# Causal attention in a fused kernel: 64x64 blocks and array tiles in place of full 128x128 blocks

## Chip, cores and metric

The kernel runs on one core of one Trainium2 chip. The metric is device time in microseconds (us), median of several runs. TensorE is called PE, VectorE DVE, ScalarE ACT, GpSimd POOL, and SyncE, which issues the DMA transfers, SP.

## What is computed

Three layers, one after the other, for 2 sequences of 768 tokens with 8 heads of 64 features. The first is linear attention with a decay gamma per head:

```python
for t in range(S):
    state = gamma * state + einsum('bhd,bhe->bhde', k[:, :, t], v[:, :, t])
    y[:, :, t] = scale * einsum('bhd,bhde->bhe', q[:, :, t], state)
```

Then a channel mix of shifted tokens, sigmoid(xr @ w_r) * (relu(xk @ w_k) ** 2 @ w_v), and a gated layer: gelu(x @ w_in), a norm over features, a token mix with w_sg, a product with the other half, and w_out, added to x. Matrix products are in fp32 precision.

## The kernel before

The sequence is cut into 6 positions of 128 tokens, for each of 2 sequences: 12 **chunks**, numbered by position first (chunk 2c + b is position c of sequence b). A chunk comes in two DMA loads of 512 KB, its query-key block (`qk`) and its key-value block (`kv`); six such blocks may be held at a time. For a chunk PE and the others do:

- `scores` (L410): per head keys times queries, 128x128 over 64 features, 8 matmuls in two row tiles of the array, into the PSUM tiles `sc`, two banks of a chunk;
- `decay` (L419): DVE multiplies both banks by a 0/1 mask that keeps a query's own and earlier keys, into `prs`; at L424 POOL (L428 DVE for the first chunks) scales the values by decay into `vs`;
- `inter` (L472): the state carried from the positions before, times the queries, 64x64 over 128 columns, 8 matmuls in four array tiles, into `y`;
- `state` (L446): keys times values, accumulated in `st` over the whole sequence, 64x64 from 128 tokens, 8 matmuls; ACT or DVE copies `st` to `sbd` (in `scr`, L241) after a pair of chunks;
- `intra` (L483): `prs` times `vs`, added to `y`, 8 matmuls over 128 keys in two column tiles.

After a pair of chunks `tokens` (L497) scales `y` into the layer's input `x`. The rest is dense: `dense` (L314 to 325) issues products of 128x128 by 512 columns, for each in three passes (high by high part, high by low, low by high), whose operands DVE and ACT split (`xo`, L241 and L311; weights, L267 to L293, from raw loads in three `raw` buffers). `kp` (w_k), `rp` (w_r) and `vp` (w_v) are the channel mix, three blocks of tokens each; a `kp` tile is 12 matmuls.

All work is entered as operations with a cost and the tiles that it reads and writes. `Plan.order` runs them in a simulated time, an engine at a time taking the earliest entered operation that is ready and whose buffers are free; the sequence that comes out is the program of every engine, SP among them, in which an instruction that waits holds those behind it. So a changed cost or buffer number reorders all engines' queues. PSUM has 8 places of one bank, `ps`, shared by scores, state, `y` and dense tiles.

## Time and profile before

| | us |
|---|---|
| median of 3 runs (368.2 to 369.91) | 368.61 |
| the profiled execution | 369.48 |
| its span, first to last instruction | 367.4 |
| PE busy | 354.3 (96%) |
| DVE busy | 246.6 (67%) |
| ACT busy | 155.4 (42%) |
| mean granted PE clock | 0.989 |

The profile is of one execution; times in it count from the span's start. A share of busy time averages over stages: up to 54 us the attention and the loading of its inputs take the time, after that the dense products. The trace views below show a stretch at a time: the busy time of each engine, the chain of work that ended last, and the instructions in order of time with the wait in front of them.

### The profile page before, as it was taken

To read this page: it belongs to the slowest core of one execution; us is meant where nothing else is said; L and a number is where in the kernel's file an instruction comes from. 1 tells how busy PE (TensorE), PEld (TensorE's weight loads), DVE (VectorE), ACT (ScalarE), POOL (GpSimd) and SP (SyncE) were. 2 spreads that over 40 slices of the span, in tenths; PEclk is the share of its full clock that TensorE was granted. 3 is DMA by queue.
4 is the path that set the end of the run, shared out by engine and by line. 5 is a ranking of instruction groups with operands and counts; after the bars stand their busy time and mean duration, and the time that the engine had idled before them with its cause. 6 is when DMAs were issued, how large, how long until landed. Compare 5 with 4: busy or idle time off the path is not lost.

```text
span 367.4 us, 5406 instructions
## 1 busy us (share of the span) xinstructions
PE 354.3 (96%) x2154; PEld 295.1 (80%) x2154; DVE 246.6 (67%) x481; ACT 155.4 (42%) x264; POOL 17.4 (5%) x19
## 2 busy tenths in 40 slices
PE   5959999999999999999999999999999999999995
PEld 2848888888888888888888888888888888899884
DVE  2779999899899895025899448669384666436422
ACT  1147538988998773006897034324133000000000
POOL 0334510000000000000000000000000000000000
PEclk9969999999999999999999999999999999999999
DMA  7999626114464025000133101110211000110032
GB/s 257 414 409 407 276 59 189 40 59 144 146 197 145 0 64 167 0 0 2 57 114 116 44 0 45 43 43 2 49 38 45 0 0 2 52 62 2 29 115 86
DMA packets 12136, 35.97 MB, mean 98 GB/s; under 512 B 1232, under 2 KB 3408, under 8 KB 12112
## 3 DMA queue, kind: packets, MB, share of 16 engines
q1 hardware_dynamic: 12112, 35.63, 28.6%
q8 instruction: 17, 0.28, 0.3%
q14 instruction: 7, 0.06, 0.1%
HBM read 32.48 MB, written 3.15 MB: 97 GB/s over the span
## 4 chain that ended last, share of the span: by engine, by line
PE 86%; DMA 7%; DVE 5%; SPq 1%; issue 0%
PE vp L322 27%; PE kp L322 18%; PE sp L322 14%; PE up L322 9%; PE rp L322 9%; PE op L322 7%; DMA chunk<-qk 3%; DMA scr<-ydec 2%; DVE prs L419 2%; DMA out<-o 2%; PE sc L410 1%; PE y L483 1%; DVE xo L311 1%; DVE o L732 1%; DVE mix L527 1%; DVE x L497 1%
## 5 line engine op out<-in xcount | busy, mean ns | idle before, releaser
L322 PE MATMUL kp<-xo,wk 128*128 128x512 f32 x288 | 66.5, 390 | 0.0
L322 PE MATMUL vp<-k,wv 128*128 128x512 f32 x288 | 65.8, 389 | 0.0
L322 PEld LDWEIGHTS kp<-xo,wk 128*128 128x128 f32 x288 | 53.8, 188 | 11.6 <-issue 0.5
L322 PEld LDWEIGHTS vp<-k,wv 128*128 128x128 f32 x288 | 54.1, 188 | 11.2
L322 PE MATMUL sp<-wsg,vh 128*128 128x512 f32 (+1 forms) x288 | 50.2, 336 | 0.0
L322 PEld LDWEIGHTS sp<-wsg,vh 128*128 128x128 f32 x288 | 44.4, 190 | 5.7
L322 PE MATMUL vp<-win,x2o 128*128 128x512 f32 x144 | 33.1, 389 | 0.0
L322 PE MATMUL up<-x2o,win 128*128 128x512 f32 x144 | 33.1, 389 | 0.0
L322 PE MATMUL rp<-xo,wr 128*128 128x512 f32 x144 | 33.1, 389 | 0.0
L322 PE MATMUL op<-gt,wout 128*128 128x512 f32 x144 | 33.0, 389 | 0.0
L322 PEld LDWEIGHTS vp<-win,x2o 128*128 128x128 f32 x144 | 27.0, 188 | 5.6
L322 PEld LDWEIGHTS up<-x2o,win 128*128 128x128 f32 x144 | 27.0, 188 | 5.6
L322 PEld LDWEIGHTS rp<-xo,wr 128*128 128x128 f32 x144 | 27.0, 188 | 5.6
L322 PEld LDWEIGHTS op<-gt,wout 128*128 128x128 f32 x144 | 27.0, 188 | 5.6
L566 DVE TENSOR_TENSOR x<-vp,x 128x512 f32<-128x512 f32 x12 | 8.3, 692 | 27.9 <-PE vp L322 27.9
L710 DVE SCALAR_TENSOR_TENSOR g<-sp,con,bsg 128x512 f32<-128x512 f32 x12 | 9.0, 752 | 23.4 <-PE sp L322 23.4
L267 ACT ACTIVATE cv<-raw 128x512 f32<-128x512 f32 x32 | 20.9, 668 | 6.5 <-DMA raw<-w_k 6.1
L289 DVE SCALAR_TENSOR_TENSOR cv<-raw,cv 128x512 int32<-128x512 int32 x32 | 22.1, 691 | 0.8
L547 ACT ACTIVATE k<-rk 128x512 fp32r<-128x512 f32 x19 | 12.0, 631 | 24.5 <-DVE rk L541 24.1
L732 DVE TENSOR_TENSOR o<-op,x 128x256 f32<-128x256 f32 (+1 forms) x20 | 8.8, 474 | 19.8 <-PE op L322 13.7
L410 PE MATMUL sc<-chunk 64*128 64x128 f32 x192 | 14.6, 296 | 7.8 <-DMA chunk<-qk 7.8
L410 PEld LDWEIGHTS sc<-chunk 64*128 64x128 f32 x192 | 12.4, 199 | 10.2 <-issue 6.1
(82 smaller groups left out, 416.9 us busy)
## 6 DMA issues: line engine op xcount, KB each, us to landing
chunk<-qk SPq DMA_DIRECT2D x12, 512.0 KB, 9.8
chunk<-kv SPq DMA_DIRECT2D x12, 512.0 KB, 10.1
raw<-w_k SPq DMA_DIRECT2D x8, 512.0 KB, 8.5
raw<-w_v SPq DMA_DIRECT2D x8, 512.0 KB, 3.5
raw<-w_in SPq DMA_DIRECT2D x8, 512.0 KB, 4.0
out<-o SPq DMA_DIRECT2D x12, 256.0 KB, 2.2
raw<-w_sg SPq DMA_DIRECT2D x6, 384.0 KB, 3.2
raw<-w_r SPq DMA_DIRECT2D x4, 512.0 KB, 4.1
```

The lines of the kernel that those rows point to most:

```text
L267: plan.op("ACT", .68, lambda: act.activation(out=xf(), in_=word(1).bitcast(F32), func=ACTF.Copy, scale=F64_REBIAS), r=[(raw, 0)], w=[(xb, ...
L289: plan.op("DVE", .69, lambda: dve.scalar_tensor_tensor(out=xi(), in0=word(1), scalar=F64_SIGN, in1=xi(), op0=ALU.bitwise_and, op1=ALU.bitw ...
L311: plan.op("DVE", .69, lambda: dve.tensor_tensor(out=lo(), in0=src(), in1=hi(), op=ALU.subtract), r=[*keep, (buf, ("hi", part))], w=[(buf, ...
L322: pe.matmul(out=T[ps][:, cols], lhsT=l(), rhs=r(), start=first and q == 0 and i == 0, stop=q == 2 and i == len(grp) - 1, skip_group_check= ...
L410: pe.matmul(out=T["sc", i, p][:, j * CH:(j + 1) * CH], lhsT=a[par[p], 1, j], rhs=a[par[p], 0, j], start=j == 0, stop=j == KD - 1, skip_gro ...
L419: plan.op("DVE", .66, lambda p=p: dve.tensor_tensor(out=T["pr", i % 4][:, p], in0=heads(T["sc", i, p]), in1=T["mask"].unsqueeze(1).to_broa ...
L483: pe.matmul(out=y_at(i, j, p), lhsT=T["vs", i][:, 2 * j + p], rhs=T["pr", i % 4][:, p, j], start=c == 0 and b == 0 and j < 2, stop=b == B ...
L497: dve.tensor_tensor(out=T[x][:, e::2, :, 1 + off:1 + off + CH], in0=T["y", c, e].rearrange("p (b j t) -> p j b t", b=B, t=CH), in1=table[: ...
L547: plan.op("ACT", .63, lambda: act.activation(out=T[o][:, 0], in_=T[rk], func=ACTF.Square), r=[(rk, 0)], w=[(o, ("hi", 0))], new=[new_p("k2 ...
L566: plan.op("DVE", .69, lambda: dve.tensor_tensor(out=T[x2][:, m], in0=T[ps], in1=T[x2][:, m], op=ALU.mult), r=[(ps, 0)], w=[(x2, m)])
L710: dve.scalar_tensor_tensor(out=out_, in0=in_, scalar=T["vec"][:, 2, m:m + 1], in1=t.unsqueeze(1).to_broadcast([128, B, BW]) if last else t ...
L732: plan.op("DVE", .69 if g == B else .42, lambda n=n, ps=ps, o=o, m=m, part=part, of=of: dve.tensor_tensor(out=T[o][:, part], in0=T[ps][:, ...
```

## The change

Of a chunk's 128x128 score block per head, a quarter (late keys for early queries) is masked away, and a quarter (early keys for late queries) is kept whole. The change computes only the other three quarters. Scores come as 16 matmuls in four 64x64 array tiles: early 64 keys with all 128 queries, late 64 keys with the late 64 queries. DVE multiplies only the first 64 columns of every block, in which the diagonal blocks lie, by a mask of 64 columns, one operation for a chunk; ACT copies the quarter that is kept whole, two copies of 64 partitions by 4x64. `intra` becomes two groups of 8 matmuls, early keys with 128 columns and late keys with 64, again in four array tiles; the host places odd tiles' values with their halves exchanged, to fit. Four tiles would write a bank from different row tiles, so `turn` puts a small operation on POOL or ACT between groups that must not overlap: it waits for the last group on `y`, and the next group waits for it. There are 11 of them, 7 on POOL and 4 on ACT. PSUM is divided anew: 4 places of one bank, and 2 of two banks for scores, which every third dense tile uses too (half of it).

```diff
 CH = 128
+HALF = CH // 2
-CONST_SHAPES = ((CH,), (NCH, H), (NCH, KD), (3, KD))
+CONST_SHAPES = ((HALF,), (NCH, H), (NCH, KD), (3, KD))
...
-    slots = {"aA": 1, "aB": 1, "bA": 1, "bB": 1, "cA": 1, "p4": 17, "raw": 3, "t": 8 + EARLY, "ps": 8, "x": NB, "small": 2}
-    plan = Plan(slots, {"p4": {"chunk": CHUNKS, "xo": XO, "k2_0": 2, "k2": 8}, "ps": {"sc": 4, "y": 2},
+    slots = {"aA": 1, "aB": 1, "bA": 1, "bB": 1, "cA": 1, "p4": 17, "raw": 3, "t": 8 + EARLY, "ps": 4, "sc": 2, "x": NB, "small": 2}
+    plan = Plan(slots, {"p4": {"chunk": CHUNKS, "xo": XO, "k2_0": 2, "k2": 8}, "ps": {"y": 2},
...
+    def new_sc(kind, buf):
+        return new("sc", kind, buf, (128, 2, 512))
...
+    homes = {}
+
+    def bank(ps):
+        return T[ps][:, 0] if homes[ps] else T[ps]
+
     def dense(kind, ps, cost, steps, first=True, cols=slice(0, 512)):
 
         n = len(steps)
+        if first:
+            homes[ps] = len(homes) % 3 == 2
+        two = homes[ps]
...
-                    new=[new_b(kind, ps)] if q == 0 and first else [])
+                    new=[(new_sc if two else new_b)(kind, ps)] if q == 0 and first else [])
...
     def scores(i):
         def go():
             a = T["qk", i]
-            for j in range(KD):
-                for p in range(2):
-                    pe.matmul(out=T["sc", i, p][:, j * CH:(j + 1) * CH], lhsT=a[par[p], 1, j], rhs=a[par[p], 0, j],
-                              start=j == 0, stop=j == KD - 1, skip_group_check=True)
-        plan.op("PE", 1.0, go, r=[(("qk", i), 0)], w=[(("sc", i, p), 0) for p in range(2)],
-                new=[new_b("sc", ("sc", i, p)) for p in range(2)])
+            for q in range(0, KD, 2):
+                for late in range(2):
+                    for j in (q, q + 1):
+                        for p in range(2):
+                            keys = slice(late * HALF, (late + 1) * HALF)
+                            pe.matmul(out=T["sc", i][par[late ^ (j & 1)], p, j * CH:(j + 1) * CH - late * HALF],
+                                      lhsT=a[par[p], 1, j, keys], rhs=a[par[p], 0, j, late * HALF:],
+                                      start=j < 2, stop=j >= 2, skip_group_check=True)
+        plan.op("PE", .68, go, r=[(("qk", i), 0)], w=[(("sc", i), 0)], new=[new_sc("sc", ("sc", i))])
...
-        for p in range(2):
-            plan.op("DVE", .66, lambda p=p: dve.tensor_tensor(
-                out=T["pr", i % 4][:, p], in0=heads(T["sc", i, p]), in1=T["mask"].unsqueeze(1).to_broadcast([128, KD, CH]),
-                op=ALU.mult), r=[(("sc", i, p), 0), ("con", 0)], w=[("prs", (i % 4, p))],
-                new=[prs_new] if i == 0 and p == 0 else [])
+        plan.op("DVE", .68, lambda: dve.tensor_tensor(
+            out=T["pr", i % 4][:, :, 0:HALF], in0=blocks(i)[:, :, 0:HALF],
+            in1=T["mask"].unsqueeze(1).to_broadcast([128, H, HALF]), op=ALU.mult),
+            r=[(("sc", i), 0), ("con", 0)], w=[("prs", (i % 4, 0))], new=[prs_new] if i == 0 else [])
+
+        def rest():
+            for odd in range(2):
+                act.copy(T["pr", i % 4][par[odd], odd::2, HALF:], blocks(i)[par[odd], odd::2, HALF:])
+        plan.op("ACT", .85, rest, r=[(("sc", i), 0)], w=[("prs", (i % 4, 1))])
...
+    def turn(c):
+        if c not in tiled:
+            return None
+
+        def go(e):
+            if e is act:
+                act.copy(T["turn"][:, 0:1], T["con"][0:1, 0:1])
+            else:
+                pool.memset(T["turn"][:, 1:2], 0.0)
+        n = plan.op("POOL ACT", (.1, .2), go, r=[(("y", c, 0), 0), ("con", 0)], w=[("turn", 0)])
+        plan.after[n] = [tiled[c]]
+        return n
...
-    def intra(i):
+    def intra(i, late, gate):
...
-            for j in range(KD):
-                for p in range(2):
-                    pe.matmul(out=y_at(i, j, p), lhsT=T["vs", i][:, 2 * j + p], rhs=T["pr", i % 4][:, p, j],
-                              start=c == 0 and b == 0 and j < 2, stop=b == B - 1 and j >= 2, skip_group_check=True)
-        plan.op("PE", .95, go, r=[(("vs", i), 0), ("prs", (i % 4, 0)), ("prs", (i % 4, 1))],
-                w=[(("y", c, e), 0) for e in range(2)], new=[] if c else y_new(i))
+            if True:
+                for q in range(0, KD, 2):
+                    for j in (q, q + 1):
+                        for p in range(2):
+                            rows = par[late ^ (j & 1)]
+                            pe.matmul(out=y_at(i, j, p)[:, late * HALF:], lhsT=T["vs", i][rows, 2 * j + p],
+                                      rhs=T["pr", i % 4][rows, KD * p + j, 0:CH - late * HALF],
+                                      start=c == 0 and b == 0 and j < 2 and not late, stop=b == B - 1 and j >= 2,
+                                      skip_group_check=True)
+        n = tiled[c] = plan.op("PE", .22 if late else .43, go, r=[("turn", 0)] * (gate is not None) + [(("vs", i), 0), ("prs", (i % 4, 0)), ("prs", (i % 4, 1))],
+                w=[(("y", c, e), 0) for e in range(2)], new=[] if c or late else y_new(i))
+        if gate is not None:
+            plan.after[n] = [gate]
...
-        for step in (scores, decay, inter, state, intra):
+        for step in (scores, decay, inter):
             for i in pair:
                 step(i)
+        for late, i in enumerate(pair):
+            state(i)
+            gate = turn(c)
+            for k in pair:
+                intra(k, late, gate)
         tokens(c)
...
+        for k in plan.after.get(i, ()):
+            tc.add_manual_dep(nc.cur_bb.bb.instructions[at], ended[k], fence, reason="row tiles on one bank")
+        ended[i] = nc.cur_bb.bb.instructions[-1].name
...
-    mask = (i[None, :] >= i[:, None]).astype(f32)
+    mask = (i[None, :HALF] >= i[:, None] % HALF).astype(f32)
```

The planner's costs change, so queues do. **SP, the first loads.** `raw<-w_k` is a weight load, `chunk<-kv` and `chunk<-qk` are blocks of chunks; the first row is chunk 3's query-key block. Before:

```order
L351 DMA chunk_150<-qk 128x1024
L248 DMA raw_152<-w_k 128x512
L248 DMA raw_155<-w_k 128x512
L248 DMA raw_157<-w_k 128x512
L354 DMA chunk_168<-kv 128x1024
L351 DMA chunk_216<-qk 128x1024
L354 DMA chunk_240<-kv 128x1024
```

With the change:

```order
L364 DMA chunk_168<-qk 128x1024
L367 DMA chunk_180<-kv 128x1024
L253 DMA raw_184<-w_k 128x512
L253 DMA raw_186<-w_k 128x512
L253 DMA raw_188<-w_k 128x512
L364 DMA chunk_222<-qk 128x1024
L367 DMA chunk_275<-kv 128x1024
```

Chunk 3's key-value block moved ahead of three weight loads.

**PE, the last position.** sc is `scores`, y<-chunk is `inter`, y<-prs is `intra`, kp a dense product of w_k. Before:

```order
L410 MATMUL sc<-chunk 128x128 x16
L472 MATMUL y<-chunk,scr_118 64x128 x16
L322 MATMUL kp<-xo,wk_284 128x512 x4
L483 MATMUL y<-prs_148,vs 64x128 x16
L322 MATMUL kp<-xo,wk_285 128x512 x4
```

With the change (the first row ends chunk 11's scores):

```order
L427 MATMUL sc<-chunk 64x64 x4
L511 MATMUL y<-chunk,scr_122 64x128 x8
L335 MATMUL kp<-xo,wk_503 128x512 x4
L525 MATMUL y<-prs_166,vs 64x128 x16
L335 MATMUL kp<-xo,wk_503 128x512 x4
L525 MATMUL y<-prs_166,vs 64x64 x16
L335 MATMUL kp<-xo,wk_504 128x512 x4
```

The late halves are a group of their own, and kp groups of four stand between the attention's groups, as they do in other positions; 32 kp matmuls come ahead of the last late group, where 8 came ahead of the last `intra` before.

**SP, the last loads of chunks, and DVE, what frees the buffer of the weight load among them.** SP before:

```order
L354 DMA chunk_507<-kv 128x1024
L351 DMA chunk_530<-qk 128x1024
L354 DMA chunk_568<-kv 128x1024
L351 DMA chunk_608<-qk 128x1024
L354 DMA chunk_619<-kv 128x1024
L248 DMA raw_681<-w_k 128x512
```

SP with the change:

```order
L364 DMA chunk_688<-qk 128x1024
L253 DMA raw_728<-w_k 128x512
L367 DMA chunk_753<-kv 128x1024
L253 DMA raw_756<-w_k 128x512
L364 DMA chunk_766<-qk 128x1024
L367 DMA chunk_776<-kv 128x1024
L253 DMA raw_873<-w_k 128x512
```

The sixth load of w_k now stands ahead of chunk 10's key-value block, the seventh ahead of both blocks of chunk 11. DVE with the change (prs<-sc is the masked product, of chunk 7 in the first row and of chunks 8 and 9 in the last; L294 is the last reader of a raw buffer):

```order
L438 TENSOR_TENSOR prs_166<-sc,con 128x8x64
L298 TENSOR_TENSOR wk_504<-cv,wk_503 128x512
L287 SCALAR_TENSOR_TENSOR cv<-cv,raw 128x512
L294 SCALAR_TENSOR_TENSOR cv<-raw,cv 128x512
L287 SCALAR_TENSOR_TENSOR cv<-cv,raw 128x512
L294 SCALAR_TENSOR_TENSOR cv<-raw,cv 128x512
L287 SCALAR_TENSOR_TENSOR cv<-cv,raw 128x512
L543 TENSOR_TENSOR x<-y,scr_123 128x2x2x128 x2
L438 TENSOR_TENSOR prs_165<-sc,con 128x8x64 x2
```

The L294 rows here free the raw buffers of w_k's third and fourth piece, for which the sixth and the seventh load wait; before, one load came between chunks 7 and 8, and the last two behind all blocks.

## Rows read from the trace of the kernel before

**Rows 1.** Stretch, busy us of PE, PEld, DVE, ACT, POOL; granted clock, DMA share, GB/s.
```profile
9.20:22.80 13.60, 9.00 (x176) 7.67 (x176) 10.49 (x15) 5.21 (x9) 4.59 (x4) 0.94 1.03 413
22.80:54.10 31.30, 30.88 (x521) 26.29 (x521) 29.27 (x45) 15.58 (x26) 12.65 (x11) 0.92 0.72 280
...
18.40:27.60 9.20, 5.13 (x56) 4.42 (x52) 7.05 (x11) 4.59 (x8) 3.21 (x3) 0.65 1.03 411
```

**Rows 2.** The chain that ended last, in order: start us, us, what.
```profile
54.11 33.79 PE kp L322 x148
87.90 10.88 PE rp L322 x48
```

**Rows 3.** Timeline of PE: start us, us, line, operation, tiles, count, idle before.
```profile
42.64 1.16 PE L410 MATMUL sc<-chunk 64*128 64x128 f32 x16
43.73 0.67 PE L472 MATMUL y<-chunk,scr 64*64 64x128 f32 x16
44.33 0.69 PE L446 MATMUL st<-vs,chunk 128*64 128x64 f32 x16
44.84 1.04 PE L483 MATMUL y<-prs,vs 128*64 128x128 f32 x16
45.72 0.63 PE L446 MATMUL st<-vs,chunk 128*64 128x64 f32 x16
...
50.98 1.20 PE L322 MATMUL kp<-xo,wk 128*128 128x512 f32 x4
52.10 2.01 PE L483 MATMUL y<-prs,vs 128*64 128x128 f32 x32
54.04 0.50 PE L322 MATMUL kp<-xo,wk 128*128 128x512 f32 x1
```

**Rows 4.** Tile views: ns of one instruction (min/median/max), first and last start.
```profile
L446 PE MATMUL st<-vs,chunk x160: 219/222/367, 10.2 to 46.1; 128*64 128x64 f32 x160
L472 PE MATMUL y<-chunk,scr x160: 269/269/443, 15.0 to 50.8; 64*64 64x128 f32 x160
L483 PE MATMUL y<-prs,vs x192: 272/273/421, 10.7 to 53.8; 128*64 128x128 f32 x192
```

**Rows 5.** Timeline of POOL (chunk 3's values) and ACT (the first w_k load).
```profile
21.55 1.09 POOL L424 TENSOR_TENSOR vs<-chunk,con 128x512 f32<-128x512 f32 x1 [6.90 <-DMA chunk<-kv]
...
16.12 0.67 ACT L267 ACTIVATE cv<-raw 128x512 f32<-128x512 f32 x1 [1.32 <-DMA raw<-w_k]
```

**Rows 6.** Timeline of PE behind the wait for chunk 4.
```profile
22.89 2.08 PE L410 MATMUL sc<-chunk 64*128 64x128 f32 x16 [4.07 <-DMA chunk<-qk]
24.90 1.12 PE L446 MATMUL st<-vs,chunk 128*64 128x64 f32 x16
25.80 1.92 PE L483 MATMUL y<-prs,vs 128*64 128x128 f32 x16
```

**Rows 7.** Timeline: a chunk's two products on DVE, and weight loads that waited for them.
```profile
45.44 1.27 DVE L419 TENSOR_TENSOR prs<-sc,con 128x512 f32<-128x512 f32 x2
...
46.77 0.85 PEld L483 LDWEIGHTS y<-prs,vs 128*64 128x64 f32 x14 [0.41 <-DVE prs L419]
```

**Rows 8.** Timeline: state on PE, its copy on ACT, carried state; POOL's shortest.
```profile
0.24 0.10 POOL L825 MEMSET const-float32-0.0<- 128x1 f32 x1 [0.24 <-issue]
...
13.48 0.69 PE L446 MATMUL st<-vs,chunk 128*64 128x64 f32 x16
...
14.21 0.59 ACT L241 COPY scr<-st 128x512 f32<-128x512 f32 x1 [12.20 <-PE st L446]
...
14.97 0.42 PEld L472 LDWEIGHTS y<-chunk,scr 64*64 64x64 f32 x16 [0.17 <-ACT scr L241]
```

**Rows 9.** Timeline of DVE: the last low part of rp's first operands.
```profile
87.52 0.69 DVE L311 TENSOR_TENSOR xo<-mix,xo 128x512 fp32r<-128x512 f32 x1
```

**Rows 10.** Timeline of SP's last two w_k loads; landing times of the chunk loads.
```profile
48.76 5.80 SPq L248 DMA_DIRECT2D raw<-w_k  x2
...
DMA to landing us min/median/max: 3.3/9.9/11.8
```

More of the change, by code (lines that the diff above doesn't have):

```diff
@@ L56, in __init__ @@
         self.ops, self.writer, self.readers, self.users, self.origin = [], {}, {}, {}, {}
-        self.slots, self.quota, self.most = slots, quota, most
+        self.slots, self.quota, self.most, self.after = slots, quota, most, {}
     def op(self, eng, cost, fn, r=(), w=(), new=(), after=()):
@@ L321, in go @@
                 for i, (_, l, _, r) in enumerate(grp):
-                    pe.matmul(out=T[ps][:, cols], lhsT=l(), rhs=r(), start=first and q == 0 and i == 0,
+                    pe.matmul(out=bank(ps)[:, cols], lhsT=l(), rhs=r(), start=first and q == 0 and i == 0,
                               stop=q == 2 and i == len(grp) - 1, skip_group_check=cols != slice(0, 512))
             plan.op("PE", cost * len(grp), go, r=[k for st in grp for k in (st[0], st[2])], w=[(ps, 0)],
-                    new=[new_b(kind, ps)] if q == 0 and first else [])
+                    new=[(new_sc if two else new_b)(kind, ps)] if q == 0 and first else [])
     def passes(pairs):
@@ L399, in omu @@
     def omu():
+        T["turn"] = cp.tile([1, 2], F32, name="turn")
         T["omu"] = cp.tile([128, 2, KD], F32, name="omu")
@@ L559, in r_tile @@
         dense("rp", ps, MM, passes([(w_view("wr", m, kk, KD), pair_view(("xo", n, kk, 1))) for kk in range(KD)]))
-        plan.op("ACT", .6, lambda: act.activation(out=T[x2][:, m], in_=T[ps], func=ACTF.Sigmoid), r=[(ps, 0)],
+        plan.op("ACT", .6, lambda: act.activation(out=T[x2][:, m], in_=bank(ps), func=ACTF.Sigmoid), r=[(ps, 0)],
                 w=[(x2, m)], new=[new("x", "x2", x2, (128, KD, BLK))] if m == 0 else [])
@@ L565, in v_tile @@
         dense("vp", ps, MM, passes([(w_view("wv", m, kk, KF), pair_view(("k2", n, kk))) for kk in range(KF)]))
-        plan.op("DVE", .69, lambda: dve.tensor_tensor(out=T[x2][:, m], in0=T[ps], in1=T[x2][:, m], op=ALU.mult),
+        plan.op("DVE", .69, lambda: dve.tensor_tensor(out=T[x2][:, m], in0=bank(ps), in1=T[x2][:, m], op=ALU.mult),
                 r=[(ps, 0)], w=[(x2, m)])
@@ L632, in c1 @@
                  (weight["win", kk], kk, lambda h, kk=kk: T[weight["win", kk]][h][:, kk % 4])) for kk in range(KD)]))
[L633 removed]
+            plan.op("ACT", .6, lambda e=e, ps=ps: act.activation(out=T[v][:, e], in_=bank(ps), func=ACTF.Gelu_apprx_tanh),
                     r=[(ps, 0)], w=[(v, e)], new=[new("raw", "raw", v, (128, 2, DM))] if e == 0 else [])
@@ L681, in c2 @@
         dense("up", ps, MM, passes([(w_view("win", KD + m, kk, KD), pair_view(("x2o", n, kk))) for kk in range(KD)]))
-        plan.op("ACT", .6, lambda: act.activation(out=view(), in_=T[ps], func=ACTF.Gelu_apprx_tanh), r=[(ps, 0)],
+        plan.op("ACT", .6, lambda: act.activation(out=view(), in_=bank(ps), func=ACTF.Gelu_apprx_tanh), r=[(ps, 0)],
                 w=[(buf, m)], new=[nw] if nw else [])
@@ L732, in c4 @@
                 plan.op("DVE", .69 if g == B else .42, lambda n=n, ps=ps, o=o, m=m, part=part, of=of: dve.tensor_tensor(
-                    out=T[o][:, part], in0=T[ps][:, part], in1=T["x2", n][:, m, of], op=ALU.add),
+                    out=T[o][:, part], in0=bank(ps)[:, part], in1=T["x2", n][:, m, of], op=ALU.add),
                     r=[(ps, 0), (("x2", n), m)], w=[(o, n)], new=[new_t("o", o)] if n != 1 else [])
@@ L756, in fused_kernel @@
         c4(g)
-    last = {}
+    last, ended = {}, {}
+    fence = mybir.DependencyInfo(mybir.DependencyClass.Sync, mybir.DependencyReason.DATA)
     edge = mybir.DependencyInfo(mybir.DependencyClass.NoSync, mybir.DependencyReason.DATA)
@@ L764, in fused_kernel @@
         e = plan.on[i]
-        plan.ops[i][2](*([{"ACT": act, "DVE": dve}[e]] if " " in plan.ops[i][0] else []))
+        plan.ops[i][2](*([{"ACT": act, "DVE": dve, "POOL": pool}[e]] if " " in plan.ops[i][0] else []))
         for ins in list(nc.cur_bb.bb.instructions)[at:]:
```

26 lines of the change are left out of this document (17 added, 9 removed).

## Prediction

> **What bounds the kernel now.** First the stretches by engine [rows 1]. From 9.2 to 22.8 us TensorE (PE) is busy 9.00 of 13.60 us, while the DMA engines are full (share 1.03, 413 GB/s). From 22.8 to 54.1 PE is busy 30.88 of 31.30 us. VectorE (DVE) is nearly full too: 29.27 of 31.30 us. Then the chain that ended last [rows 2]: from 54.11 on it is PE alone, 148 kp matmuls in 33.79 us, then rp, 48 in 10.88 us, so 0.227 us each. What PE waited for before 22.89 is the query-key block of chunk 4, for 4.07 us [rows 6]. The change leaves these dense matmuls as they are. The kernel is therefore as long as the moment at which dense work starts, less what kp work is already done by then: 8 of 156 kp matmuls before 54.1. All that the change is worth is decided between 22.8 and 54.1 us.
>
> **What a group costs there.** Attention groups follow each other on PE without pause, so I read them by their starts [rows 3]. Every matmul of the code is two instructions in the trace, so 8 are "x16". Starts to starts: scores (L410) 42.64 to 43.73, 1.09 us; carried state times query (L472) 0.60; state (L446) about 0.5; masked product times value (L483) 44.84 to 45.72, 0.88 us, and for a pair 52.10 to 54.04, 0.97 each: 0.925 on average. Taking the duration of one instruction [rows 4] (scores' as that of the masked products, both have 128 columns) off the stretch of 16 and dividing by 15 gives the pace of starts: scores (1.16-0.272)/15 = 59 ns; masked products (1.04-0.273)/15 = 51 ns; state (0.69-0.222)/15 = 31 ns; carried state, which already uses all four 64x64 tiles, (0.67-0.269)/15 = 26.7 ns. Two tiles at 51 and four at 26.7 ns, both with 128 columns: the pace halves as tiles double. What is over 16 paces is the entry into a group, 0.14 us for scores, 0.17 for carried state; I use 0.15.
>
> **The new groups.** Scores and masked products of a chunk each become 16 matmuls, 32 instructions: 16 with 128 moving columns at 26.7 ns, and 16 with 64. No row shows 64 columns on four tiles. The nearest is the state group, 64 columns on two tiles: its 31 ns against 51 for 128 columns is a factor of 0.61, which makes 16.3 ns. The bounds are 13.4 (half of 26.7) and 26.7 (no shorter). So 0.427 + 0.261 + 0.15 = 0.84 us a chunk for each kind (bounds 0.79 and 1.00). Of the chunks with scores after 22.8 (4 to 11): scores 8 x (1.09-0.84) = **2.0 us less**, masked products 8 x (0.925-0.84) = **0.7 us less**.
>
> **What moves.** The planner reorders the queues. On SP the value block of chunk 3 now stands before the first three w_k loads. In the row of before it landed at about 21.5, when POOL's 6.90 us wait ended, while the w_k load in its future place had landed at 16.1 [rows 5]. If landings keep the order of issue, as these two do, chunk 3's state and masked product, now at 24.90 and 25.80, run before chunk 4 lands. That takes 0.50 + 0.925 = **1.4 us** out of the stretch (in the rows they took 1.12 and 1.92, as the clock was at 1.2 GHz [rows 6]; I assume that chunk 4 and 5 take over that loss). On PE 32 kp matmuls instead of 8 stand before the last masked product. They are a credit of 24 x 0.227 = 5.4 us, but come in six more groups of four, each 50.98 to 52.10, 1.12 us [rows 3], against 0.91 at the dense pace: **1.3 us more** for switching. Twice the second masked product of a pair stopped after its first two instructions, its weight loads idle for 0.41 us until DVE's product was there; one of the two is shown [rows 7]. By the new order other groups stand ahead of these: **0.8 us less**.
>
> **What is added.** Eleven fences, nine of them after 22.8: PE's last y matmul, an empty operation on POOL or ACT, PE again. The nearest round trip is state, ACT copy, carried state [rows 8]: 0.04 us from PE's end to ACT's start, 0.17 from ACT's end to PE's weight load. With a POOL memset of 0.10 us a fence takes 0.31 us after PE's end, while a state group of 0.5 or a longer group runs in between. I take **0.3 us more** for all. If that cover fails (POOL is in a value scaling of 1.09 us [rows 5]) the four fences with only a state group could lose up to 1.1 us each, 4.4 us. ACT's 16 copies of 64x256 in the stretch cost between half of and a whole 128x512 copy, 0.30 to 0.59 us [rows 8], 4.7 to 9.4 us beside 15.58 busy of 31.3: they fit. They stand behind DVE's product of the same chunk, so the way from scores to masked product is 0.64 + 0.6 to 1.2 us where two products took 1.27 [rows 7]; carried state (0.60) and a kp group (1.12) usually cover it. DVE loses 8 products of 0.64, 5.1 us, so it isn't the end. The dense tiles now share 4 + 2 PSUM places instead of 8: a kp tile takes PE 12 x 0.227 = 2.7 us and its evacuation, taken as ACT's copy of that size, 0.59 [rows 8], so six places are many and I take nothing; were they not enough, gaps in dense work would show it.
>
> **The sum**: -2.0 -0.7 -1.4 +1.3 -0.8 +0.3 = **3.3 us less**. Dense work then begins at 54.1 - 3.3 + 5.4 = 56.2 us with 32 kp matmuls behind it. The profiled execution takes 369.48 us (span 367.4 and 2.1 around it) and would take 366.2. The median of the runs is 368.61, 0.9 lower, so I give **365.3 us**. Does dense work outrun its operands? Before, the last low part that rp's first tile reads starts at 87.52 [rows 9] and rp at 87.90 [rows 2], so DVE and ACT are hardly ahead there. But by the new order DVE has done four more operations of such a size (0.69) when the attention ends, two low parts of w_k, one other conversion and one low part of a square: 2.8 us, nearly the gain. I take no stall; one of 2.6 us would end where (a) does.
>
> **Rivals.**
> (a) *Half-length matmuls are no shorter on four tiles.* Then 26.7 ns for all: 16 groups x 0.16 = 2.6 us back, **367.9 us** (365.3 + 2.6), no change that a measurement can tell (under about 0.5%, 1.8 us, none can). For it: no row with four tiles and 64 columns. Against it: the state group, whose 64 columns are paced by two tiles' work. The Trainium skill, TensorE: Matmul & The Clock Gate, section "Wait — 56ns, not 53.3ns?", says that starts never come closer than about 25 ns however few the columns; by it the half-length starts would cost 25 ns and the sum would be 1.1 us less instead of 3.3, an estimate of 367.5 us. No run here yet shows which. Chance 0.2.
> (b) *The clock stays up.* PE waited 4.07 us before chunk 4, and the granted clock of that stretch is 0.65 [rows 1, 6]: the scores behind it took 2.08 instead of 1.16, masked products 1.92 instead of 1.04, state 1.12 instead of 0.69, 2.2 us lost. With chunk 3 done in that idle time the gap shrinks by about 1.4 us. If the clock doesn't fall, 2.2 more are gained: **363.1**, and 362.3 with half-length starts at 13.4 ns. Against it: gaps remain, and DMA still sets them. Chance 0.2.
> (c) *Slower: chunk loads stuck behind weights on SP.* The sixth and seventh w_k loads now stand before the last query-key and value blocks. A w_k load waits until a raw buffer is converted: the seventh was issued at 48.76, the eighth at the end of the same 5.80 us, so about 54.2 [rows 10]; there both stood behind all chunk loads. If the seventh again goes at 48.8, chunk 11's block lands at the earliest 3.3 us (the shortest landing [rows 10]) after an issue at 49.2, 52.5; then scores 0.84, carried state 0.60, kp 1.12, masked products 1.0, kp 1.12 and the late halves 0.7 make dense work start at 57.9: 367.0. Each us later costs one; from 50.4 on nothing is gained, and at 54.2, the eighth's time, it is 3.8 us slower: **372.4**. Against it: by the new order DVE runs the conversion that frees this buffer between the products of chunk 7 and chunk 8, not behind all products. Chance 0.12, with the fences' 4.4 us in it.
>
> **How the numbers follow.** Forecast 0.48, (a) 0.2, (b) 0.2, (c) 0.12. Faster: 0.48 + 0.2 = 0.68; same 0.2; slower 0.12. The range runs from (b) with the shorter starts, 362.3, to (a) with a little of the fences' cost, 368.3; it leaves out most of (c) and a better end than (b).
>
> **What would show it.** Right: scores of a chunk as 32 instructions within about 0.95 us; POOL scaling chunk 3's values at 16 to 17 us instead of 21.55; 32 kp matmuls by the last masked product and gapless dense work from 55 to 57 us; rp starting about 3 us earlier than 87.90. Wrong: score groups at 1.0 us or more (a), a granted clock of 1.0 from 18 to 28 us (b), PE waiting for chunk 10 or 11 with SP in a wait for DVE (c), PE idle for POOL or ACT after state groups (the fences), or new gaps in kp and rp after 57 us (operands or PSUM places).

## Result: 1 per cent slower, and the profile after

```
                       median us (lowest to highest, runs)   profiled run   span    granted clock
before                 368.61 (368.2 to 369.91, 5)           369.48         367.4   0.989
changed                371.79 (371.16 to 372.85, 5)          371.68         369.8   0.991
ratio 1.0102, 95% interval 1.0067 to 1.0138
```

The forecast was 365.3 us. All of the loss lies ahead of rp, as the chain of work that ended last shows (the view of [rows 2], now of the changed kernel; start us, us, what):

```profile
60.68 12.02 PE kp L335 x52
77.10 13.21 PE kp L335 x57
90.31 10.88 PE rp L335 x48
```

rp starts at 90.31 instead of 87.90, 2.41 us later, and the span is 2.4 us longer. Dense work begins at 60.68, not at 56.2, with the 32 kp matmuls behind it that the forecast gave it, and PE stops in it once, for 1.01 us before 77.10.

The new groups cost what was forecast or less. Below is the timeline of PE in the changed kernel (the view of [rows 3]; start us, us, line, tiles, count, idle before). Scores start 0.72 us before the next group (36.77 to 37.49), against 1.09 before and 0.84 forecast:

```profile
21.93 0.40 PE L525 MATMUL y<-prs,vs 64*64 64x64 f32 x12 [1.22 <-issue]
...
24.29 0.90 PE L427 MATMUL sc<-chunk 64*64 64x128 f32 x32 [0.46 <-DMA chunk<-qk]
25.00 0.62 PE L511 MATMUL y<-chunk,scr 64*64 64x128 f32 x16
26.71 0.69 PE L470 MATMUL st<-vs,chunk 128*64 128x64 f32 x16 [1.09 <-POOL turn L498]
28.40 0.85 PE L525 MATMUL y<-prs,vs 64*64 64x128 f32 x14 [1.01 <-ACT prs L445]
...
34.24 0.86 PE L511 MATMUL y<-chunk,scr 64*64 64x128 f32 x16 [0.64 <-ACT scr L246]
...
36.77 0.90 PE L427 MATMUL sc<-chunk 64*64 64x128 f32 x32
37.49 0.62 PE L511 MATMUL y<-chunk,scr 64*64 64x128 f32 x16
...
45.40 1.09 PE L511 MATMUL y<-chunk,scr 64*64 64x128 f32 x28 [0.96 <-DVE x L543]
...
52.67 0.27 PE L427 MATMUL sc<-chunk 64*64 64x64 f32 x2 [1.50 <-issue]
...
77.10 13.21 PE L335 MATMUL kp<-xo,wk 128*128 128x512 f32 x57 [1.01 <-DVE xo L246]
```

So the time went into waits. By stretches (columns as in [rows 1]), first the changed kernel, then the kernel before:

```profile
9.20:90.31 81.11, 72.36 (x1213) 58.27 (x1207) 67.89 (x101) 58.67 (x113) 19.15 (x22) 0.96 0.61 222
...
28.40:33.60 5.20, 5.14 (x112) 4.40 (x112) 5.03 (x8) 4.70 (x10) 1.10 (x2) 0.67 0.94 354
```

```profile
9.20:87.90 78.70, 73.67 (x845) 61.94 (x846) 70.71 (x109) 50.77 (x87) 17.24 (x15) 0.96 0.61 227
...
22.89:27.66 4.77, 4.77 (x49) 4.22 (x49) 3.63 (x7) 1.20 (x2) 2.18 (x2) 0.50 1.04 411
```

Up to rp PE works 1.31 us less (73.67 to 72.36) and idles 3.72 us more (5.03 to 8.75). Of the 5.03 before, 4.69 were waits for chunk blocks; of the 8.75 only 0.46.

A point to compare is the scores of chunk 5, with the same groups done ahead of them in both kernels. They start at 24.29 in the changed kernel and here before:

```profile
28.36 1.16 PE L410 MATMUL sc<-chunk 64*128 64x128 f32 x16
```

There the change is 4.07 us ahead. (The kernel before has its slow-clock stretch behind it then, granted 0.50; the changed one has its own still ahead, 0.67 from 28.40 on.) From there to rp it takes 66.02 us against 59.54, so it loses 6.48: six waits of 1.09, 1.01, 0.64, 0.96, 1.50 and 1.01, together 6.21, where the kernel before had 0.34, and 0.6 of work. Which waits, and why, is what the runs ask.

### The profile page after: what moved, and what is told of

Read it like the earlier page. It is cut to its first block, busy times and chain, and to the rows that moved or that the text cites. A ratio compares the mean times of both kernels' runs of the same rounds, so it can differ in the third digit from the quotient of the medians.

```text
span 369.8 us, 6197 instructions
## 1 busy us (share of the span) xinstructions
PE 353.6 (96%) x2538; PEld 291.6 (79%) x2538; DVE 242.7 (66%) x473; ACT 162.4 (44%) x288; POOL 19.4 (5%) x26
## 4 chain that ended last, share of the span: by engine, by line
PE 89%; DVE 3%; DMA 3%; issue 2%; ACT 1%; SPq 0%; DVEq 0%; ACTq 0%
PE vp L335 26%; PE kp L335 17%; PE sp L335 13%; PE up L335 9%; PE rp L335 9%; PE op L335 7%; PE y L525 3%; PE sc L427 2%; DMA chunk<-qk 2%; DMA out<-o 2%; PE st L470 1%; PE y L511 1%; DVE o L783 1%; DVE x L543 1%; DVE cv L287 1%
## 5 line engine op out<-in xcount | busy, mean ns | idle before, releaser
L335 PE MATMUL kp<-xo,wk 128*128 128x512 f32 x288 | 68.2, 393 | 1.0 <-DVE xo L246 1.0
L294 DVE SCALAR_TENSOR_TENSOR cv<-raw,cv 128x512 int32<-128x512 int32 x32 | 23.5, 734 | 0.6
L601 DVE TENSOR_TENSOR k<-rk,k 128x512 fp32r<-128x512 f32 x19 | 13.1, 689 | 8.1 <-ACT rk L600 7.9
L287 DVE SCALAR_TENSOR_TENSOR cv<-cv,raw 128x512 int32<-128x512 int32 x22 | 16.8, 762 | 1.8 <-ACT raw L280 1.8
```

The costliest lines, as they stand in the source:

```text
L287: dve.scalar_tensor_tensor(out=xi(), in0=xi(), scalar=3, in1=word(0), op0=ALU.logical_shift_left, op1=ALU.bitwise_or)
L294: plan.op("DVE", .69, lambda: dve.scalar_tensor_tensor(out=xi(), in0=word(1), scalar=F64_SIGN, in1=xi(), op0=ALU.bitwise_and, op1=ALU.bitw ...
L335: pe.matmul(out=bank(ps)[:, cols], lhsT=l(), rhs=r(), start=first and q == 0 and i == 0, stop=q == 2 and i == len(grp) - 1, skip_group_che ...
L601: plan.op("DVE", .69, lambda: dve.tensor_tensor(out=T[o][:, 1], in0=T[rk], in1=T[o][:, 0], op=ALU.subtract), r=[(rk, 0), (o, ("hi", 0))], ...
```

## The theories

- **A**: the way scores, DVE product, ACT copies, masked product is long, and the planner doesn't know that the copies wait for the product. They do, as the trace shows, but the planner's table has no such edge. (Both read one PSUM place and write one `prs` buffer; no run shows which of the two orders them.)

```profile
ACT prs L445 <- DVE prs L438: 16.4, 7, 6.9
```

  This row of ACT's waits gives us in total, times, longest. The longest, 6.89 us up to 8.92, lies at the start, when ACT has no other work; the other six are 9.5 us.
- **C**: waits marked "issue" have no semaphore behind them. By this theory they are PE's own code arriving late. The changed kernel has 384 more matmuls (2538 against 2154) and as many more weight loads, and the page's queue of code loads has 20 packets, in the kernel before 17 (packets, MB, share):

```profile
q8 instruction: 20, 0.33, 0.4%
```

  In the trace's records of DMA packets each of these has 16,384 bytes.
- **D**: six PSUM places are too few, but for y, not for dense tiles: beside the state only three of the four single places are left, and a pair of chunks takes two, so the next pair waits until DVE has read the last (1.70 us in two places).
- **B**: the order of loads on SP. **E**: the fences. **G**: DVE's load.

What led to these, in one place of the changed kernel, in the timelines of ACT, POOL and DVE:

```profile
15.34 0.76 ACT L445 COPY prs<-sc 64x256 f32<-64x256 f32 x2 [1.21 <-DVE prs L438]
18.09 0.76 ACT L445 COPY prs<-sc 64x256 f32<-64x256 f32 x2 [1.99 <-DVE prs L438]
18.87 0.68 ACT L272 ACTIVATE cv<-raw 128x512 f32<-128x512 f32 x1
...
23.79 1.42 POOL L456 TENSOR_TENSOR scr<-scr,con 128x512 f32<-128x512 f32 x1 [3.75 <-DVE x L543]
25.17 1.49 POOL L448 TENSOR_TENSOR vs<-chunk,con 128x512 f32<-128x512 f32 x1
...
22.43 1.29 DVE L543 TENSOR_TENSOR x<-y,scr 128x512 f32<-128x512 f32 x2 [1.69 <-PE y L525]
23.63 0.68 DVE L294 SCALAR_TENSOR_TENSOR cv<-raw,cv 128x512 int32<-128x512 int32 x1
24.23 1.53 DVE L287 SCALAR_TENSOR_TENSOR cv<-cv,raw 128x512 int32<-128x512 int32 x1
25.79 1.41 DVE L294 SCALAR_TENSOR_TENSOR cv<-raw,cv 128x512 int32<-128x512 int32 x1
27.13 0.68 DVE L438 TENSOR_TENSOR prs<-sc,con 128x512 f32<-128x512 f32 x1
```

The first w_k conversion starts on ACT at 18.87 (16.12 before [rows 5]). About half of that delay is the order on SP: the load, now behind chunk 3's values, lands at 17.52 instead of 16.10. The rest is ACT, which stands 1.99 us with copies at the head of its queue. PE's masked product of chunk 3 stops for 1.22 us without a semaphore, so DVE gets to its tokens only at 22.43. Behind the tokens stand POOL's scaling, and so the state at 26.71; and DVE's belated conversions, and so the product of chunk 4 at 27.13, its copies, and PE's wait that ends at 28.40. So by this chain one stop on PE comes back as two more waits. Two of the conversions take 1.53 and 1.41 instead of 0.68 us, while POOL works.

## Experiments

All times and ratios are beside runs of the kernel before on the same chip. The runs are spread over five chips, so runs with different values of "before" are best compared by their ratios. The last column is what PE waits without a semaphore after 30 us in the profiled run, in us.

```
run                       median   before   ratio (95% interval)      "issue" after 30 us
PSUM divided, rest before 370.37   368.15   1.0076 (1.0044-1.0109)    0
plan told                 370.50   368.15   1.0085 (1.0052-1.0118)    2.40
copies left out           371.31   368.15   1.0115 (1.0077-1.0152)    0.46
code moved by 64          369.88   368.15   1.0063 (1.0037-1.0089)    0
the change again          371.99   367.91   1.0120 (1.0080-1.0160)    1.16
single banks, told        373.53   367.91   1.0166 (1.0126-1.0207)    3.58
w_k loads held            373.05   367.91   1.0141 (1.0099-1.0182)    0
single banks, told, held  372.02   367.91   1.0125 (1.0089-1.0161)    0.46
told, moved by 64         369.92   368.27   1.0044 (1.0015-1.0072)    0
told, moved by 96         372.93   368.27   1.0125 (1.0080-1.0171)    2.71
change, half conversions  370.48   368.27   1.0067 (1.0036-1.0098)    2.38
before, half conversions  366.69   368.27   0.9971 (0.9940-1.0002)    0
scores only               367.70   368.02   1.0012 (0.9985-1.0040)    1.59
scores untrimmed          369.90   368.02   1.0074 (1.0045-1.0102)    0
scores only, moved by 64  367.57   368.02   1.0012 (0.9987-1.0037)    0
longer fences             372.01   367.37   1.0140 (1.0095-1.0186)    0.40
scores only, moved by 32  367.35   367.37   1.0002 (0.9977-1.0028)    0.95
```

**The change again, as a control.** No edit.

> The changed kernel once more, beside the others of this call: 371 to 372.5 us, 1.010 of before. If it is 370 or less, the gains of the earlier runs against 371.8 were the chip's and not the edits'.

371.99 us: the loss is that of the kernel, not of a chip.

**PSUM divided, on the kernel before.**

```diff
-"ps": 8
+"ps": 4, "sc": 2
-out=T["sc", i, p][:, j * CH:(j + 1) * CH]
+out=T["sc", i][:, p, j * CH:(j + 1) * CH]
```

> The kernel before with one thing of the change alone: PSUM as 4 single places and 2 of two banks, scores of a chunk in one two-bank place, dense tiles sharing 4 + 2 places. Theory A (the loss of the change comes from the way scores, DVE product, ACT copies, masked product, in queues ordered by a plan that doesn't know that the copies wait for the product): 368.6 us, within 1 us, rp starts at 88 +- 0.7, no gap in dense work that the kernel before lacks. Rival D (six places are too few): 370 to 372 us, with waits of kp, rp or scores for a PSUM place.

D holds, and not where the forecast looked. Every engine runs the same operations in the same order as in the kernel before; beside the places, only DVE's first product differs, which now waits for both banks of the scores. The timeline of PE has a new wait of 3.27 us of carried state for DVE's tokens (the earlier pair's y still unread), and dense work has none:

```profile
24.55 0.44 PE L482 MATMUL y<-chunk,scr 64*64 64x128 f32 x4
28.25 0.65 PE L482 MATMUL y<-chunk,scr 64*64 64x128 f32 x12 [3.27 <-DVE x L507]
```

The first four instructions go into the one free place, the rest waits. This edit alone costs 0.76 per cent (0.44 to 1.09), where the whole change costs 1.0 to 1.2.

**Plan told.** Only the planner's table changes.

```diff
-plan.op("ACT", .85, rest, r=[(("sc", i), 0)], w=...)
+plan.op("ACT", .85, rest, r=[(("sc", i), 0), ("prs", (i % 4, 0))], w=...)
```

> The changed kernel, with the plan alone told that ACT's two copies wait for DVE's product of that chunk, so that it places them and the work behind them anew; every instruction stays the same. Theory A: the time in which ACT stands before the copies for DVE falls from 16.4 us to under 8, conversions run earlier, the stall of kp at 72 to 77 us (1.0) goes, and the kernel takes 369 to 370.5 us. Rival A2 (the way through DVE and ACT is itself too long, whatever stands in the queues) and rival C (the loss is PE's code loads that land late): within 0.9 of 371.8.

ACT's wait ahead of its copies falls from 16.4 to 13.7 us, or, without the first wait at the start, from 9.5 to 7.6. The fall to under 8 that was expected compares with these 9.5:

```profile
ACT prs L445 <- DVE prs L438: 13.7, 8, 6.1
```

In the chain the stop at 77 us is gone, and rp starts 1.87 us earlier:

```profile
58.30 30.15 PE kp L335 x132
88.44 10.88 PE rp L335 x48
```

The median is 370.5 us, 1.5 under the change, though PE's second stop without a semaphore grew to 2.07 us. The ratios (1.0085 against 1.0102 and 1.0120) make it 0.6 to 1.3 us, and their intervals overlap. A holds for a part, on the traces more than on the times.

**Copies left out** (from chunk 4 on).

```diff
-for odd in range(2):
+for odd in range(2 if i < 4 else 0):
```

> The changed kernel without ACT's copies from chunk 4 on: the plan still reckons with them, so the order of all queues is the same; the masked products then read what chunks 0 to 3 left there for the full blocks, so that part of the output is not computed. Theory A: PE's wait of 1.0 us for the copies at 28.4 us and DVE's 2.8 us for them go, ACT doesn't stand for DVE's products, dense work starts 1.5 to 3 us before 60.68 and the kernel takes 368.5 to 370.5 us. Rival C (late code loads on PE, 1.5 and 1.2 us): these two stalls stay, at most 0.7 us faster than 371.8. Rival B (the last chunk loads stand behind w_k loads on SP): PE waits for chunk 10 or 11 as soon as the rest is earlier, dense work not before 60.

Mostly a miss for A: 371.31, no measurable gain. The waits of PE show why:

```profile
PE y L511 <- DVE x L543: 3.8, 3, 2.1
...
PE y L525 <- DVE prs L438: 1.2, 2, 0.6
```

Masked products now wait for DVE itself, and y's wait for a PSUM place grew from 1.7 to 3.8 us. The way through ACT was one of several that end close together; taking it away lets D end last. In the profiled run dense work did begin 1.56 us earlier (59.12); that run is the fastest of six.

**Code moved.** 64 short matmuls in the warm-up, 128 PE instructions.

```diff
+for _ in range(64):
+    pe.matmul(out=T["warmps"][:, :8], lhsT=T["warm"][:, :128], rhs=T["warm"][:, :8], start=True, stop=True)
```

> The changed kernel with 64 more warm-up matmuls of 8 columns, 128 PE instructions, which is half of a 16 KB piece of code; order and data stay the same. Theory C (the two stalls of PE in which no semaphore is waited for, 1.43 us at 20.74 and 1.7 us at 51.2, are late code loads): the stalls leave these two instructions and come 128 PE instructions earlier in the program or go; the time changes by up to 1.5 us either way. Rival (the stalls belong to these instructions, whatever the code's place): they stay at the same matmuls, masked product of chunk 2 and scores of chunk 10, and the time is 371.8 +- 0.9.

```profile
20.50 1.09 PE L527 MATMUL y<-prs,vs 64*64 64x128 f32 x29 [0.77 <-issue]
...
26.79 0.78 PE L429 MATMUL sc<-chunk 64*64 64x128 f32 x25 [1.94 <-issue]
```

The stops left their matmuls: the late half of chunk 3's product and chunk 10's scores run through; the early products of chunks 2 and 3 and chunk 5's scores stop instead. The same instructions, data and order take 2 us less (1.4 to 2.1 by the ratios). With the plan told and two amounts:

> The changed kernel with the plan told of the copies' wait, and with the 64 short warm-up matmuls. Theory C: PE's stalls without a semaphore come at its weight loads 349 and 477, as with the shift alone, and not near 984; the gains of the two runs (1.5 from the plan, 2 from the shift) come from different waits and add: 368 to 369.5 us. Rival (they cover each other, since DVE's conversions for kp and rp set the end): 369.5 to 370.5.

> The same with 96 short warm-up matmuls instead of 64. Theory C: stalls again at weight loads 349 and 477 (or 605 and others 128 apart), but now 32 matmuls further ahead in the program, so with other sizes; 368 to 370.5 us. Rival (stalls belong to fixed instructions): the time equals that with 64 within 0.5 and the stalls keep their matmuls.

369.92 and 372.93, on one chip: 32 short matmuls more in the warm-up cost 3 us. With 64 the stops came where C put them, but the two gains do not add: 369.92 lies in the rival's range, and the first kp group now waits 1.06 us for a part of w_k. With 96 the time is 2.4 us above C's range, and PE stops five times:

```profile
19.04 0.65 PE L513 MATMUL y<-chunk,scr 64*64 64x128 f32 x12 [1.15 <-issue]
...
25.18 0.44 PE L429 MATMUL sc<-chunk 64*64 64x128 f32 x8 [1.91 <-issue]
...
37.97 0.51 PE L429 MATMUL sc<-chunk 64*64 64x128 f32 x13 [1.89 <-issue]
50.29 0.99 PE L527 MATMUL y<-prs,vs 64*64 64x128 f32 x27 [0.23 <-issue]
55.12 0.44 PE L429 MATMUL sc<-chunk 64*64 64x128 f32 x8 [0.59 <-issue]
```

The number of the matmul that came late, counted in the trace from the first one (warm-up included):

```
the change                    349 (masked product of chunk 3), 984 (scores of chunk 10)
the change again              349, 603, 984
plan told                     350, 603, 985 (the last now carried state)
copies left out               349, 984
code moved by 64              350, 477
told, moved by 64             350, 478
told, moved by 96             351, 478, 731, 985, 1113
single banks, told            349, 602, 727, 854
w_k loads held                349
single banks, told, held      349, 727
change, half conversions      349, 984
longer fences                 349, 984
scores only                   223, 732
scores only, moved by 32      732
```

Whatever matmul stands there, the stops lie on one scale, one step of which is 125 to 128 matmuls: with their weight loads and a few semaphore instructions, 256 instructions. The trace's records of DMA packets settle C. In the change one packet of code is under way from 19.54 to 20.65 us and PE goes on at 21.93; another from 50.33 to 51.33, and PE goes on at 52.67. In all 33 stops of this table PE goes on 1.20 to 1.62 us after the end of a packet of code. The Trainium skill, Runtime: NRT & Kernel Launch, section "Instruction fetch mechanics", says that an engine's code is fetched by DMA in blocks of 16 KiB, 256 instructions, and that crossing a block costs little, being mostly hidden. The blocks agree with the trace; that it is hidden does not: a crossing cost up to 2.38 us (half conversions, DMA share 0.95 in that stretch).

**w_k loads held** behind the last chunk blocks.

```diff
-after=plan.writer[("kv", 1), 0])
+after=[*plan.writer[("kv", 1), 0], *(plan.writer[("kv", 11), 0] if key == ("wk", 5) else [])])
```

> The changed kernel with the sixth and all later w_k loads placed behind the last chunk's value block on SP. Theory C: in 46 to 54 us the DMA engines have less to do, the code piece that PE needs at its weight load 984 comes in time, that stall (1.5 us) is gone while the one at 349 (1.2 us) stays; 369.5 to 371 us if the later w_k doesn't stall kp. Rival B (SP order is what costs): PE waits for no chunk block after 47 us and dense work begins before 59, 368 to 369.5. Rival (neither): 371.8 or more, since the last w_k pieces come later and kp waits for them at 72 to 77 us by more than 1 us.

As C said, the stop at 984 is gone and the one at 349 stays (1.74). As its last line said, kp pays: 

```profile
77.09 8.29 PE L335 MATMUL kp<-xo,wk 128*128 128x512 f32 x28 [1.84 <-ACT xo L246]
```

Dense work begins 2.65 us earlier (58.03), with fewer kp behind it, and rp 1.64 us later (91.95). 373.05 us is no gain. So B in its simple form falls: chunk loads behind w_k loads cost no more than the w_k loads held. They may bear on C: in the change the second stop falls while they are under way (DMA share 0.99 from 49.5 to 52.7 us), and with the w_k loads held it is gone.

**Single banks.** The changed kernel with the PSUM of the kernel before, scores and products by bank, and the plan told of the copies' wait; then with the w_k loads held as well.

```diff
-"ps": 4, "sc": 2
+"ps": 8
-new=[new_sc("sc", ("sc", i))]
+new=[new_b("sc", ("sc", i, p)) for p in range(2)]
```

> The changed kernel with the PSUM of the kernel before, 8 single places: scores of a chunk in two single banks, so DVE takes its product in two of 128x4x64 and ACT its copies in four of 64x2x64; dense tiles share all places again; the plan knows that copies wait for products, as in the run that told it so. Theory D (a chunk pair's y can't begin before DVE has read the pair before, as only three places are left beside the state): y's waits for DVE's tokens go, 0.7 to 1 us in each of two places, and it takes 368.5 to 370 us against 370.5 with the plan told alone. Rival C (late code loads, PE stalls at its weight loads 349 and 984 or at another multiple of 128 from there): these stay and the time is 370 to 371.5.

> Both of the last two together: single PSUM banks, plan told, w_k loads behind the last chunk. If the waits for PSUM places, the second code stall and the order on SP each cost what their waits show (1.7, 1.5 and up to 1 us), 367 to 368.5 us, no slower than before; if they cover each other, 369 to 370.5.

y's waits for DVE's tokens are gone, as D says, but it got no faster: 373.53, and 372.02 with the loads held, both above every range that was expected. In the first PE stops three times for its code after 30 us:

```profile
34.80 0.32 PE L508 MATMUL y<-chunk,scr 64*64 64x128 f32 x1 [0.28 <-issue]
...
41.39 0.43 PE L522 MATMUL y<-prs,vs 64*64 64x128 f32 x4 [1.55 <-issue]
47.14 0.39 PE L467 MATMUL st<-vs,chunk 128*64 128x64 f32 x5 [1.75 <-issue]
```

And ACT's 48 smaller copies take 12.4 us where 24 took 8.8. The gains of the single edits don't add.

**Half conversions.** DVE's two bit operations on w_k and w_r on half the columns, in both kernels.

```diff
-out=xi(), in0=word(1), ... in1=xi()
+out=xi()[:, :256], in0=word(1)[:, :256], ... in1=xi()[:, :256]
```

> The changed kernel with DVE's two bit operations on each piece of w_k and w_r done on 256 of 512 columns, 24 operations of which about 0.33 us each is left out; order, transfers and PE work stay the same, the other columns of the weights are not computed. Theory G (in the changed kernel DVE's queue is the bound: PE waits on its products, tokens and low parts): products come earlier, the stall of kp at 72 to 77 us goes, dense work begins 1.5 to 3 us earlier, and it takes 367.5 to 369.5 us. Rival C (code loads and DMA landings decide): at most the 1.0 us of the kp stall, 371 us.

> The same lightening of DVE in the kernel before. If PE is its bound from 22.8 us on, as its PE row says (30.88 of 31.30 busy): within 0.7 of before, rp still at 87.9 +- 0.5. If DVE bounds it as well: 1 us or more faster.

Both are 1 to 2 us faster (ratio 1.0067 instead of 1.0102 and 1.0120; 0.9971), but neither is clear of noise: the first interval overlaps that of the change, the second reaches 1. The stop of kp (1.0 us) stayed, against G. If DVE's load is a part, it is one in either kernel and doesn't explain the difference.

**Longer fences.**

```diff
+for _ in range(4):
     pool.memset(T["turn"][:, 1:2], 0.0)   # or the copy on ACT
```

> The changed kernel with four empty operations in a row at each of the 11 fences instead of one: 0.3 us longer on POOL, 0.6 us on ACT. Theory (fences are covered by the state or other groups between, except where POOL's value scaling stands behind one): the time stays within 0.7 of the changed kernel's, ratio to before 1.010 to 1.013. Rival E (each fence is on the way to the end): 11 x 0.3 us and more, 3 us slower than the changed kernel, ratio 1.018 or above.

372.01, as the change. E in full, 3 us more (ratio 1.018), doesn't show, at 1.0140 (1.0095 to 1.0186); a cost of 0.7 to 1.4 us, the difference of the ratios, isn't excluded.

**Scores alone**, on the kernel before: the scores are trimmed and in four tiles, with three PSUM places of their own; the masked products stay whole, and there are no copies on ACT and no fences.

```diff
-for j in range(KD):
-    for p in range(2): ... lhsT=a[par[p], 1, j], rhs=a[par[p], 0, j]
+for q in range(0, KD, 2):
+    for late in range(2): ... lhsT=a[par[p], 1, j, keys], rhs=a[par[p], 0, j, late * 64:]
-"ps": 8
+"ps": 5, "sc": 3
```

> Half of the change, on the kernel before: scores trimmed and in four tiles, masked products whole as before, so no copies on ACT and no fences; DVE masks all 128 columns from three PSUM places kept for scores (the part never written stays zero from the warm-up); state, y and kp share the five others. 192 more matmul instructions than before instead of 384, and as many weight loads. Theory C: scores save 8 x 0.37 = 3.0 us between 22.8 and 54.1, code pieces are used up more slowly than in the changed kernel, stalls without a semaphore sum up to less than 1 us: 365 to 367.5 us. Rival G2 (DVE, 29.27 of 31.30 busy in the kernel before, is next: what PE saves is lost in waits for DVE's products and tokens): 367.5 to 369 us, with waits of masked products for DVE over 1.5 us.

> The first of this call with the 64 short warm-up matmuls. Theory C: if stalls show in the first, they move by 64 weight loads here, and the time of the two differs by what they sum up to; 365 to 368 us. If no stall shows in either, both times agree within 0.7.

> Scores alone trimmed and in four tiles, with 32 short warm-up matmuls. Theory C: a stall without a semaphore, if there is one, stands at weight load 223, 349, 477, 605, 731 or 850 give or take 4, counted with the 32, as in the runs before; time 367 to 368.5 us by how much of it falls after 30 us. If it stands elsewhere, the code-piece reading of these stalls is wrong.

367.35 to 367.70 us, at or up to 0.5 us under the kernel before, ratios 1.0002 to 1.0012 with 1 in each interval: 4 us better than the change, no measurable gain on before. The scores are as short as in the change, but PE then waits for chunk blocks, three times between 18 and 33 us, and for code (0.54 us at 16.27, 1.59 at 42.78); moved by 64 it has no such stop, moved by 32 one, on the expected scale:

```profile
22.06 0.90 PE L423 MATMUL sc<-chunk 64*64 64x128 f32 x32 [3.64 <-DMA chunk<-qk]
29.73 1.17 PE L423 MATMUL sc<-chunk 64*64 64x128 f32 x26 [0.75 <-DMA chunk<-qk]
32.28 0.90 PE L423 MATMUL sc<-chunk 64*64 64x128 f32 x32 [0.82 <-DMA chunk<-qk]
...
42.78 0.98 PE L498 MATMUL y<-prs,vs 128*64 128x128 f32 x14 [1.59 <-issue]
```

The profiled run's rp is at 85.85, 2 us earlier than in [rows 2], but the medians count: runs of the kernel before lay between 364.85 and 370.35 us in all, and its profiled run (369.48) in the upper part.

**Scores untrimmed**, on the kernel before with its eight PSUM places: four tiles, 16 matmuls of 128 columns for a chunk.

```diff
-for j in range(KD):
-    for p in range(2): ... lhsT=a[par[p], 1, j], rhs=a[par[p], 0, j]
+for q in range(0, KD, 2):
+    for late in range(2): ... lhsT=a[par[p], 1, j, keys], rhs=a[par[p], 0, j]
```

> The kernel before with scores in four tiles but not trimmed: 16 matmuls of 128 columns for a chunk instead of 8, so about the same PE time (32 instructions at 26.7 ns against 16 at 59, and 0.15 for the entry in both: 1.0 against 1.09 us) with twice the instructions for scores; PSUM, DVE and ACT as before. Theory C: stalls without a semaphore appear at weight loads 128 apart, up to 1.5 us in sum, 367.5 to 370 us. Rival (the stalls come from what else the change does): none appears, 367 to 368.5 us.

A miss for C: no stop without a semaphore, and yet 369.9. The loss is another: a masked product waits for DVE, as a DVE operation ahead of its product takes 1.56 us.

```profile
39.37 0.43 PE L491 MATMUL y<-prs,vs 128*64 128x128 f32 x2 [1.92 <-DVE prs L425]
```

So more instructions alone don't make stops; from 9.2 to 22.8 us this kernel ran 288 weight loads, the changed one 346, the kernel before 176. How fast PE may use up its code before it stops, no run measures.

## Why the prediction was wrong

The groups came out as forecast or shorter. What failed are the steps that put waits at nothing or took them as covered.

- **The groups** (-2.0 for scores): 8 x 0.37 = 3.0 by the rows after; the size was too cautious, and half-length matmuls are shorter, against rival (a). Of the 0.72 us from 36.77 to 37.49, 0.57 remain for 32 starts when the entry of 0.15 is taken off: 18 ns each. In the trace's records of this group the starts come in fours, 6 to 7 ns apart; from one four to the next it is about 109 ns with 128 columns and 57 with 64, so half the columns take about half the time. Masked products took 0.77 to 0.84 us a chunk at the full clock, as forecast or less. The Trainium skill's 25 ns (TensorE: Matmul & The Clock Gate, "Wait — 56ns, not 53.3ns?"), which the forecast set beside rival (a), don't hold between four tiles. The clock fell all the same, only later (0.67 from 28.40 on).
- **"The dense tiles now share 4 + 2 PSUM places ... I take nothing."** A failed step. It counted dense tiles; y of two neighbouring pairs needs four places and had three. On the kernel before this alone costs 2.2 us (370.37 against 368.15).
- **The number of PE instructions** had no term at all, a failed step: "scores and masked products of a chunk each become 16 matmuls, 32 instructions" was priced by starts alone. The two stops are 2.72 us in the profile, and moving the code changed the time by -2 and, with the plan told, by +3 us.
- **"Carried state and a kp group usually cover"** the way from scores to masked product. A failed step: PE waited 1.01 us, and ACT 9.5 us ahead of its copies behind the first one, which with the later loads put w_k's conversions off. This edge was missing in the plan; with it 1.5 us came back by the medians, 0.6 to 1.3 by the ratios, not clear of noise.
- **"DVE loses 8 products of 0.64, so it isn't the end."** A failed step: the sum of its work said nothing of when it came. DVE's operations came later (busy 6.77 us from 9.2 to 22.8, against 10.49 in [rows 1]) and 13.00 of 13.20 us from there to 36.
- **"I take no stall"** of dense work: a failed step of 1.01 us, at 77.10; gone in all three runs where the plan was told with the change's PSUM.
- **Fences, 0.3 us**: three more empty operations in each changed nothing that can be told from noise. **Rival (c)**, slower through SP's order: the right sign and the wrong cause, and that its 372.4 lies near the result is luck. Chunk 11's query-key block did land 8 us later than before (52.69 against 44.38), but PE reached it after that, at 55.43, and with the w_k loads held it got no faster.
- Chunk 3 was right: its values were scaled at 17.85 instead of 21.55 [rows 5], and its groups ran ahead of chunk 4. That is most of the 4.07 us by which the change led at 24.29 us.

How the 6.5 us between forecast and result divide stays open: the waits stand in for each other (copies out, and the PSUM wait grows; PSUM apart, and code stops grow). Shown by runs clear of noise are 2.2 for PSUM places on the kernel before and 2 for the code's place, each by itself; the 1.5 for the plan's missing edge is likely, not shown.

## What to carry to other kernels

A faster group of work is worth no more than the slack of what it waits for: before shortening PE work, count for each group the buffers, the queue position and the instructions that it takes, and look for the wait that is second in line. Splitting matmuls doubles PE's code, and while DMA is full a block of 256 instructions can come late; stops without a semaphore that keep a fixed distance in instructions are the sign, and a few empty matmuls ahead show it. Tell a planner every wait that the program really has, here the copies' wait for another engine's product of the same scores.

## What had not been expected of the hardware

- PE stops of 0.23 to 2.38 us where a block of code ends, while transfers run (DMA share 1.03 from 9.2 to 22.8 us in the change); each ends 1.20 to 1.62 us after a packet of code has landed.
- Matmuls of 64 columns on four tiles: a score group of 32 instructions in 0.72 us, half of them with 128 columns, with starts in fours 6 to 7 ns apart.
- DVE operations with two operands in SBUF of 1.4 to 1.6 us beside POOL's, 0.68 to 0.75 alone.
- Runs of one kernel 5 us apart (364.85 to 370.35), at granted clocks of 0.984 to 0.998; what sets them is open.
